# Attention-probability transposes by key block, and a new place for the text branch's small steps

## The chip, the cores and the metric

The kernel runs on one core of a Trainium2 chip. The metric is the device time of one execution in microseconds, the median over runs.

## What is computed

Two batches of 256 image tokens and 32 text tokens, width D = 1152, all in bf16. Each stream is normalised, scaled and shifted by rows that come from a condition vector, projected to Q, K and V with weights of its own, attended jointly over 288 keys with one head, projected out, gated and added to its input. Cut to what matters:

```
mod_i = (silu(c) @ wmod_img)   # six parts; the first three are used: shift, scale, gate
mod_t = (silu(c) @ wmod_txt)
hi = layernorm(x_img) * (1 + sci) + shi
ht = layernorm(x_txt) * (1 + sct) + sht
qkvi, qkvt = hi @ wqkv_img, ht @ wqkv_txt
q, k, v = [concatenate(text part, image part) for each]
p = softmax(q @ k.T * D**-0.5)
a = p @ v
out_i = x_img + gai * (a[image rows] @ wo_img)
out_t = x_txt + gat * (a[text rows] @ wo_txt)
```

## The kernel before

**Weights.** The fourteen weight blocks of 1152 x 1152 (2.65 MB each) pass through five slots of on-chip memory, `w0` to `w4`. A block that takes over a slot is loaded once all readers of the block before it are through, in the order of SyncE's queue (line 110 on). From the image scale on the order is: image scale (slot 0), image V (1), image shift (2), image Q (3), text shift (0), the text tokens, image K (4), text scale (1), text Q (2), four small `svb` loads, text K (3), image gate (0), text V (1), image O (4), text gate (3), text O (1). SyncE hands a DMA in only when its wait is over, and everything later in its queue stands behind it. `load_rows` hands in a block in pieces of rows, so that its first rows can be used before the last have landed.

**TensorE's order** is the order in which the program is written, since every matmul and transpose goes through `mm` or `tr`, which pin it. After the normalisation of the image tokens it is: image V, the image shift, the Shift-times-V rows (`shift_v_rows`: what the image shift contributes to V, as a row, added after attention as a bias), then image Q in nine column blocks and image K in nine (`qk_img`, 81 matmuls each). Text work hangs in hooks between those blocks: the text statistics and the text shift on VectorE, the transposes of the text tokens before K's second block, the text scale rows before K's fifth, text Q before K's ninth. Then come text K, the scores, the image gate row, text V, the transposes of P, attention, and the output.

**Shift-times-V rows.** `shift_v_rows` (line 403) makes 36 matmuls with image V's weights, ScalarE copies the rows to `svr` and stores them to a scratch in DRAM with two DMAs of its own; VectorE transposes them to columns (`svc`, the bias of the image part). Four DMAs of SyncE read the scratch back, broadcast over partitions, to `svb`, which text V's result subtracts.

**P and its transposes.** The softmax writes five tiles of 384 columns: two query tiles for each batch, and one for the text queries of both batches. VectorE writes the first 288 columns, GpSimd a second copy of the text keys further right, so that they come out on the partitions where text V's rows lie. `p_transposes` (line 628) is called for one batch and one or two key blocks at a time. It turns three tiles for each key block; for batch 1 the text tile is multiplied with `ident2`, an identity rotated by 32, since the text rows there stand first. ScalarE copies blocks 0 and 1, VectorE block 2, each into a tile of its own for each batch.

**Attention** (`attn_pair`, line 657) works on three column blocks of both batches at a time: the image keys of the first batch, the text keys of both, the image keys of the second.

**The output** has four image tiles of 128 tokens, three column chunks each (the last tile four), and one text tile. For each chunk VectorE multiplies by the gate from PSUM (`tmp`, two buffers) and adds the input. The text gate row (`txt_gate`) stands between the first and second chunk of image tile 1; it goes through ScalarE, a DRAM scratch and GpSimd's DMAs to `gbf`. The text tile (`out_txt`) stands before image tile 3.

Of the kernel before, what the change touches and what calls it, by code (L numbers as in the profile page):

```python
# [9 lines left out]
ALU = mybir.AluOpType  # L10
# [4 lines left out]
def kernel(  # L15
# [14 lines left out]
    nc = tc.nc  # L30
    bf = mybir.dt.bfloat16
    f32 = mybir.dt.float32
    PSUM = bass.MemoryType.PSUM

    B, NI, D = x_img.shape
    NT = x_txt.shape[1]
    P = 128
# [22 lines left out]
    def mm(*a, **k):  # L60
        return pin(nc.tensor.matmul(*a, **k))  # L61

    def tr(*a, **k):
        return pin(nc.tensor.transpose(*a, **k))  # L64
# [19 lines left out]
    def load_w(slot, src, c0, splits=(D,)):  # L84
        t = wtile(slot)
        sv = wview(src, c0)
        o = 0
        for n in splits:
            nc.sync.dma_start(t[:, :, o:o + n], sv[:, :, o:o + n])
            o += n  # L90
        return t

    def load_rows(slot, src, c0, cuts=(0, 3, 6)):
        t = wtile(slot)
        sv = wview(src, c0)
        for r0, r1 in zip(cuts, cuts[1:] + (KT,)):
            nc.sync.dma_start(t[:, r0:r1, :], sv[:, r0:r1, :])
        return t
# [14 lines left out]
    w_sh_t = load_rows(0, wmod_txt, 0, (0, 1, 3, 6))  # L113
    nc.sync.dma_start(x_t[:], xt_flat[:, :])
    w_k_i = load_w(4, wqkv_img, D)
    w_sc_t = load_w(1, wmod_txt, D)
    w_q_t = load_w(2, wqkv_txt, 0)

    nc.scalar.preload_act_table_set("natural_log_exp_and_others")
    eps_t = eps_row[:, 0:1]  # L120
# [27 lines left out]
    nc.gpsimd.memset(pb_txt, 0.0)  # L148
    nc.gpsimd.memset(xn_t[NTT:P, (KT - KH) * P:KH * P], 0.0)
    nc.gpsimd.memset(pb_all[:, 0:2 * B, NTOK:PBW], 0.0)  # L150
    ident2 = const.tile([P, P], bf)
    nc.gpsimd.tensor_copy(ident2[:, 0:P - NT], ident[:, NT:P])
    nc.gpsimd.tensor_copy(ident2[:, P - NT:P], ident[:, 0:NT])
    fold = const.tile([P, NGG, LW], bf)
    nc.vector.reduce_max(fold[:, 0, :], ident[:].rearrange("p (g l) -> p l g", g=NGG), axis=AX.X)
    nc.gpsimd.tensor_copy(fold[:, 1:NGG, :], fold[:, 0, :].unsqueeze(1).to_broadcast([P, NGG - 1, LW]))
# [228 lines left out]
    def qk_img(wq, blk, hooks):  # L385
        for j in range(KT):
            for hook in hooks.get(j, ()):
                hook()
            ps = ps_mm.tile([P, B * NI], f32, tag="mm")
            for kt in range(KT):  # L390
                mm(ps[:], lhsT=wq[:, kt, j * P:(j + 1) * P], rhs=hT_i[:, kt, :],
                   start=(kt == 0), stop=(kt == KT - 1))
            qk_evac(qkT[:, blk * KT + j, :, 0:NI], ps[:].rearrange("p (b n) -> p b n", b=B), blk)
# [9 lines left out]
    def shift_v_rows():  # L403
        p_sv = mod_rows_of(w_v_i, shT32)
        nc.scalar.copy(svr[:], p_sv[:])
        cols["v"] = mod_cols_of(p_sv, "svc")
        for b in range(B):
            nc.scalar.dma_start(svd[b].rearrange("(c g l) -> g c l", g=NGG, l=LW), svr[b:P:LW])
        for g in range(2):
            for b in range(B):  # L410
                r0 = 64 * g + NT * b
                nc.sync.dma_start(svb[r0:r0 + NT, :], svd[b, g * HD:(g + 1) * HD].partition_broadcast(NT))
# [84 lines left out]
    def qk_txt(blk, wq):  # L497
        for j0 in range(0, KT, FG):
            jn = min(FG, KT - j0)
            ps = ps_mm.tile([P, FG, NTT], f32, tag="mm")  # L500
            for j in range(j0, j0 + jn):
                for kt in range(KT):
                    mm(ps[:, j - j0, :], lhsT=wq[:, kt, j * P:(j + 1) * P], rhs=hT_t[:, kt, :],
                       start=(kt == 0), stop=(kt == KT - 1))
            qk_evac(qkT[:, blk * KT + j0:blk * KT + j0 + jn, :, NI:NTOK],
                    ps[:, 0:jn, :].rearrange("p j (b n) -> p j b n", b=B), blk)
# [52 lines left out]
    def txt_gate():  # L559
        mod_row_out(mod_rows(w_ga_t), 1)  # L560
        for g in range(2):
            for b in range(B):
# [2 lines left out]
                                    gsc[1, b, :].rearrange("(r g j) -> g r j", r=2, g=2)[g].partition_broadcast(NT))  # L565

    v_last()
    shift_v_rows()
    w_k_t = load_w(3, wqkv_txt, D)
    w_ga_i = load_w(0, wmod_img, 2 * D)  # L570
    w_v_t = load_w(1, wqkv_txt, 2 * D)
    w_o_i = load_rows(4, wo_img, 0)
    w_ga_t = load_w(3, wmod_txt, 2 * D)
    w_o_t = load_rows(1, wo_txt, 0, (0, 5))
    qk_img(w_q_i, 0, {0: (shift_part(0, 2),), 3: (txt_stats, shift_part(2, 4), txt_var, txt_norm),
                      5: (shift_part(4, 7),), 8: (shift_part(7, KT),)})
    qk_img(w_k_i, 1, {1: (txt_transposes,), 4: (txt_rows_scale, shift_blocks, txt_scale),
                      7: (shift_fold, txt_shift), 8: (lambda: qk_txt(0, w_q_t),)})
    qk_txt(1, w_k_t)

    aT = act.tile([P, KT, B * NTOK], bf, tag="Q")
    qpos = [[0, P, 2 * P], [NT, NT + P, 0]]
# [17 lines left out]
    def soft_div(key):  # L600
        sps, qn, nmx, e, rs = soft[key]
        pin(nc.vector.reciprocal(rs[0:qn, :], rs[0:qn, :]))  # L602
        pb = pb_txt if key == "t" else pb_tiles[key[0] * TPB + key[1]]
        pin(nc.vector.tensor_scalar_mul(pb[0:qn, 0:NTOK], e[0:qn, :], rs[0:qn, :]))
        pin(nc.gpsimd.tensor_scalar(pb[0:qn, NI + 2 * NT:NI + 3 * NT], e[0:qn, NI:NTOK], rs[0:qn, :], 0.0,  # L605
                                     op0=ALU.mult, op1=ALU.add))
        pbs[key] = pb

    def scores_img(b, qi):
# [13 lines left out]
                   start=(ft < 2), stop=(ft >= KT - 2), tile_position=(0, r0))  # L623
        return sps

    pTs = {}

    def p_transposes(b, kjs, pool, copy):
        pT_ps = pool.tile([P, 8 * P], bf, tag="tr" if pool is ps_tr else "mm", name="pT_ps")
        txt = [(2, pbs["t"], ident2 if b else ident)]  # L630
        img = [(qi, pbs[(b, qi)], ident) for qi in range(TPB)]
        for n, kj in enumerate(kjs):
            for qi, pb, perm in (txt + img if b else img + txt):
                o = n * NTOK + qpos[b][qi]
                k0 = kj * P - (NT * b if kj == 2 else 0)
                tr(pT_ps[:, o:o + P], pb[:, k0:k0 + P], perm[:])
        if b not in pTs:
            pTs[b] = work.tile([P, 3, NTOK], bf, tag="pT", name="pT")
        pin(copy(pTs[b][:, kjs[0]:kjs[-1] + 1, :],  # L639
                 pT_ps[:, 0:len(kjs) * NTOK].rearrange("p (k n) -> p k n", n=NTOK)))  # L640

    def attn_keys(tiles, first):
        for b, dt in tiles:
            for kj in range(2):
                mm(tiles[(b, dt)][:], lhsT=v_i[:, b * TPB + kj, dt * P:(dt + 1) * P], rhs=pTs[b][:, kj, :],
                   start=(first and kj == 0), stop=(not first and kj == 1))

    def attn_evac(tiles):
        for b, dt in tiles:
# [44 lines left out]
    gate_row()  # L694
    v_txt_out(0, vt[0])
    vt.append(v_txt(1))
    p_transposes(0, (0, 1), ps_tr, nc.scalar.copy)
    v_txt_out(1, vt[1])
    p_transposes(0, (2,), ps_mm, nc.vector.tensor_copy)
    p_transposes(1, (2,), ps_mm, nc.vector.tensor_copy)  # L700
    p_transposes(1, (0, 1), ps_tr, nc.scalar.copy)
    img_gate_spread()
    for dts in ((0, 5, 1), (6, 2, 7), (3, 8, 4)):
        attn_pair(*[[(b, dt) for dt in dts] for b in range(B)])

    def out_img(i, chunks, parts=None, between=None):
        b = i // TPB
        t0 = b * NTOK + qpos[b][i % TPB]
        o = work.tile([P, D], bf, tag="o")
        c0 = s0 = 0  # L710
        for n in chunks:
            if c0 and between:
                between = between()
            ps = ps_mm.tile([P, CH], f32, tag="mm")
            for dt in range(KT):
                mm(ps[:, 0:n], lhsT=aT[:, dt, t0:t0 + P], rhs=w_o_i[:, dt, c0:c0 + n],
                   start=(dt == 0), stop=(dt == KT - 1))
            tmp = work.tile([P, CH], bf, tag="tmp")
            nc.vector.tensor_mul(tmp[:, 0:n], ps[:, 0:n], gb[:, b, c0:c0 + n])  # L719
            nc.vector.tensor_add(o[:, c0:c0 + n], tmp[:, 0:n], x_i[:, i, c0:c0 + n])  # L720
            c0 += n
            if parts is None and c0 == D or parts and c0 in parts:
                (nc.scalar if parts and c0 == D else nc.sync).dma_start(oi_v[b, i % TPB, :, s0:c0], o[:, s0:c0])
                s0 = c0

    def out_txt():
        of = work.tile([P, 2, VC], bf, tag="of", bufs=1)
        for r in range(2):
            ps = ps_mm.tile([P, VC], f32, tag="mm")
            for dt in range(KT):  # L730
                for g in range(2):
                    c0 = (2 * r + g) * VC
                    mm(ps[64 * g:64 * g + NTT, :], lhsT=aT[:, dt, NI:NI + NTT], rhs=w_o_t[:, dt, c0:c0 + VC],
                       start=(dt == 0), stop=(dt == KT - 1), tile_position=(0, 64 * g))
            tmp = work.tile([P, CH], bf, tag="tmp")
            nc.vector.tensor_mul(tmp[:, 0:VC], ps[:], gbf[:, r, :])
            nc.vector.tensor_add(of[:, r, :], tmp[:, 0:VC], xf[:, r, :])
        for g in range(2):
            eng = nc.sync if g == 0 else nc.scalar
            eng.dma_start(ot_flat.rearrange("t (r g j) -> g t r j", r=2, g=2)[g], of[64 * g:64 * g + NTT, :, :])  # L740

    C3 = (CH, CH, CH)
    out_img(0, C3)
    out_img(1, C3, between=txt_gate)
    out_img(2, C3)
    out_txt()
    out_img(3, (CH, CH, 224, 160), parts=(2 * CH, D - 160, D))


# [28 lines left out]
```

## Time and profile before

| What | Value |
|---|---|
| median of 15 runs | 117.96 us (117.7 to 118.53) |
| profiled execution, its own time | 118.04 us |
| its span | 115.84 us |
| TensorE busy | 110.3 us (95% of the span) |
| VectorE busy | 72.1 us (62%) |
| ScalarE busy | 44.2 us (38%) |
| GpSimd busy | 12.4 us (11%) |
| moved by DMA | 41.02 MB, 354 GB/s over the span |

The span runs from the first to the last instruction of the profiled execution; its own time is 2.2 us longer, for what lies around it. Idle time of an engine costs nothing unless the last instruction waits for it in the end. Where one says that a transfer lands, it is the time at which the last of its DMA engines reports.

### The profile page before, as it was taken

To read this page: it belongs to the slowest core of one execution; us is meant where nothing else is said; L and a number is where in the kernel's file an instruction comes from. 1 tells how busy PE (TensorE), PEld (TensorE's weight loads), DVE (VectorE), ACT (ScalarE), POOL (GpSimd) and SP (SyncE) were. 2 spreads that over 40 slices of the span, in tenths; PEclk is the share of its full clock that TensorE was granted. 3 is DMA by queue.
4 is the path that set the end of the run, shared out by engine and by line. 5 is a ranking of instruction groups with operands and counts; after the bars stand their busy time and mean duration, and the time that the engine had idled before them with its cause. 6 is when DMAs were issued, how large, how long until landed. Compare 5 with 4: busy or idle time off the path is not lost.

```text
span 115.8 us, 2586 instructions
## 1 busy us (share of the span) xinstructions
PE 110.3 (95%) x1081; PEld 63.5 (55%) x1081; DVE 72.1 (62%) x152; ACT 44.2 (38%) x92; POOL 12.4 (11%) x34
## 2 busy tenths in 40 slices
PE   4998899999999999999999999999999999999990
PEld 2245544445674444445454458887866565557670
DVE  3489691063869999999996040018758509566671
ACT  5799800041752289825241233244657400100000
POOL 7300000000000000000000000003431600424000
PEclk9999999999999999999999999999999999999998
DMA  3999999999999999999999999999999999953223
GB/s 108 372 383 385 396 404 409 415 412 408 413 400 411 309 383 403 411 412 409 414 350 388 410 407 411 410 410 408 410 407 409 403 426 366 393 192 51 102 51 102
DMA packets 18917, 41.02 MB, mean 354 GB/s; under 512 B 1323, under 2 KB 1851, under 8 KB 18907
## 3 DMA queue, kind: packets, MB, share of 16 engines
q1 hardware_dynamic: 18032, 39.85, 89.9%
q0 software_dynamic: 480, 0.89, 2.5%
q10 hardware_dynamic: 395, 0.12, 0.4%
q8 instruction: 8, 0.13, 0.4%
q14 instruction: 2, 0.02, 0.0%
HBM read 39.52 MB, written 1.34 MB: 353 GB/s over the span
## 4 chain that ended last, share of the span: by engine, by line
PE 84%; ACT 5%; DVE 4%; DMA 3%; issue 1%; DVEq 0%
PE ps L61 52%; PE vps L61 15%; PE gps L61 5%; PE aps L61 5%; PE sps L61 4%; DMA x_i<-in_x_img_dram 3%; ACT xn_i L198 2%; ACT xn_i L197 2%; DVE tmp L719 1%; DVE xT_i L260 1%; DVE o L720 1%; PE tp L64 1%; ACT pT L639 1%; PE sc_ps L61 1%; DVE xn_i L212 0%
## 5 line engine op out<-in xcount | busy, mean ns | idle before, releaser
L61 PE MATMUL ps<-xT_i,t 128*128 128x512 bf16 x162 | 35.7, 379 | 0.0
L61 PEld LDWEIGHTS <-t 128*128 128x128 bf16 x333 | 20.9, 98 | 19.1 <-issue 0.7
L453 DVE SCALAR_TENSOR_TENSOR acc_sh<-t,sTf,acc_sh 128x1152 f32<-128x1152 bf16 x16 | 21.4, 1405 | 0.0
L61 PE MATMUL ps<-t,aT 128*128 128x384 bf16 (+3 forms) x153 | 20.3, 308 | 0.0
L61 PE MATMUL vps<-t,hS_i 128*128 128x512 bf16 (+1 forms) x108 | 17.9, 326 | 0.5 <-DVE scc L265 0.5
L61 PEld LDWEIGHTS <-aT 128*128 128x128 bf16 (+1 forms) x153 | 13.0, 101 | 7.1 <-issue 0.8
L61 PEld LDWEIGHTS <-hS_i 128*128 128x128 bf16 x108 | 9.1, 98 | 9.2 <-issue 0.5
L719 DVE TENSOR_TENSOR tmp<-ps,gb 128x384 bf16<-128x384 f32 (+2 forms) x13 | 6.8, 525 | 7.9 <-PE ps L61 4.3
L383 ACT CAST qkT<-ps 128x512 bf16<-128x512 f32 (+2 forms) x11 | 6.1, 552 | 14.8 <-PE ps L61 13.5
L605 POOL TENSOR_SCALAR pb<-e,rs 128x32 bf16<-128x32 f32 (+1 forms) x5 | 2.2, 445 | 75.8 <-DVE rs L602 75.8
L381 ACT ACTIVATE qkT<-ps 128x512 bf16<-128x512 f32 (+2 forms) x11 | 6.1, 561 | 8.3 <-PE ps L61 6.7
L61 PE MATMUL wps<-warm 128*128 128x512 bf16 x24 | 7.7, 479 | 1.5 <-DVE unit L127 1.5
L180 DVE CAST v_i<-vps 128x512 bf16<-128x512 f32 x5 | 3.5, 692 | 8.3 <-PE vps L61 8.3
L590 DVE TENSOR_REDUCE nmx<-sps 128x1 f32<-128x288 f32 x4 | 1.8, 457 | 9.4 <-PE sps L61 9.4
L182 ACT CAST v_i<-vps 128x512 bf16<-128x512 f32 x4 | 2.3, 580 | 10.3 <-PE vps L61 10.3
L652 DVE TENSOR_SCALAR aT<-aps,svc 128x288 bf16<-128x288 f32 x9 | 4.3, 517 | 2.2 <-PE aps L61 2.2
L61 PEld LDWEIGHTS <-sT 128*32 128x32 bf16 x180 | 4.5, 96 | 1.8 <-issue 1.2
L61 PEld LDWEIGHTS <-warm 128*128 128x128 bf16 x25 | 2.6, 114 | 5.0 <-issue 2.4
L61 PE MATMUL sps<-qkT 128*128 128x288 bf16 (+1 forms) x54 | 5.3, 287 | 0.0
L61 PE MATMUL gps<-t,sT 128*32 128x288 bf16 x144 | 5.2, 287 | 0.0
L61 PE MATMUL aps<-pT,v_i 128*128 128x288 bf16 x36 | 5.1, 287 | 0.1
L61 PE MATMUL ps<-hT_t,t 128*128 128x64 bf16 x162 | 5.0, 193 | 0.0
(114 smaller groups left out, 105.6 us busy)
## 6 DMA issues: line engine op xcount, KB each, us to landing
t<-in_wqkv_txt_dram SPq DMA_DIRECT2D x3, 2592.0 KB, 19.7
t<-in_wmod_img_dram SPq DMA_DIRECT2D x2, 2592.0 KB, 14.5
t<-in_wmod_txt_dram SPq DMA_DIRECT2D x2, 2592.0 KB, 18.8
t<-in_wqkv_img_dram SPq DMA_DIRECT2D x3, 864.0 KB, 13.5
t<-in_wqkv_img_dram SPq DMA_DIRECT2D x1, 2592.0 KB
t<-in_wo_img_dram SPq DMA_DIRECT2D x3, 864.0 KB, 10.4
t<-in_wqkv_img_dram SPq DMA_DIRECT2D x3, 576.0 KB, 10.6
t<-in_wmod_txt_dram SPq DMA_DIRECT2D x2, 864.0 KB, 13.0
```

The source lines that it names most:

```text
L61: return pin(nc.tensor.matmul(*a, **k))
L180: nc.vector.tensor_copy(out_ap, in_ap)
L182: nc.scalar.copy(out_ap, in_ap)
L197: pin(nc.scalar.activation(junk, x_ap, ACT.Copy, scale=1.0 / D, accum_out=sm[:, 0:1]))
L198: pin(nc.scalar.activation(junk, x_ap, ACT.Square, scale=float(D) ** -0.5, accum_out=sm[:, 1:2]))
L381: nc.scalar.mul(out_ap, in_ap, SCALE)
L383: nc.scalar.copy(out_ap, in_ap)
L453: pin(nc.vector.scalar_tensor_tensor(acc, w_sh_t[:, kt, :], col, acc, op0=ALU.mult, op1=ALU.add))
L590: pin(nc.vector.reduce_max(nmx[0:qn, :], sps[0:qn, :], axis=AX.X, negate=True))
L605: pin(nc.gpsimd.tensor_scalar(pb[0:qn, NI + 2 * NT:NI + 3 * NT], e[0:qn, NI:NTOK], rs[0:qn, :], 0.0, op0=ALU.mult, op1=ALU.add))
L652: nc.vector.tensor_scalar(dst, tiles[(b, dt)][:], bias, None, op0=ALU.add)
L719: nc.vector.tensor_mul(tmp[:, 0:n], ps[:, 0:n], gb[:, b, c0:c0 + n])
```

## The change

- **P's transposes** are made for one key block and both batches at a time, in one tile of 576 columns; the text tile is turned once for both batches, so that there are 15 and no `ident2`. Batch 1's first image tile overwrites the spare columns beside the text rows. For this the text tile holds its text keys three more times.
- **Copies** of the turned P go by batch halves: key block 0 of batch 0 by VectorE, block 1 of batch 0, then blocks 0 and 1 of batch 1 by ScalarE, block 2 as a whole by VectorE after the second text V result. In the first attention step the matmuls go over the key blocks first.
- **Shift-times-V rows** move from before image Q to before image K's fourth block, with the text scale rows, which come one block earlier. The slots change: text scale 2, text Q 3, text K 1, text V 2. Text K stands before the four `svb` loads in SyncE's queue; the image gate and what follows stand behind them. Text O comes in pieces of seven and two row blocks.
- **Text gate and text output** come after image tile 1: gate row, then the text matmuls in four column groups of 32 instead of two of 64, over the first seven row blocks of both halves and then the last two, into two PSUM tiles of the other pool. Their multiplications follow image tile 2, and GpSimd makes the two additions. VectorE's operations of the output are pinned in program order.

```diff
-    w_sc_t = load_w(1, wmod_txt, D)
-    w_q_t = load_w(2, wqkv_txt, 0)
+    w_sc_t = load_w(2, wmod_txt, D)
+    w_q_t = load_w(3, wqkv_txt, 0)
+    w_k_t = load_w(1, wqkv_txt, D)
...
-    shift_v_rows()
-    w_k_t = load_w(3, wqkv_txt, D)
-    w_ga_i = load_w(0, wmod_img, 2 * D)
-    w_v_t = load_w(1, wqkv_txt, 2 * D)
-    w_o_i = load_rows(4, wo_img, 0)
-    w_ga_t = load_w(3, wmod_txt, 2 * D)
-    w_o_t = load_rows(1, wo_txt, 0, (0, 5))
+    def late_loads():
+        late["ga_i"] = load_w(0, wmod_img, 2 * D)
+        late["v_t"] = load_w(2, wqkv_txt, 2 * D)
+        late["o_i"] = load_rows(4, wo_img, 0)
+        late["ga_t"] = load_w(3, wmod_txt, 2 * D)
+        late["o_t"] = load_rows(1, wo_txt, 0, (0, 7))
...
-    qk_img(w_k_i, 1, {1: (txt_transposes,), 4: (txt_rows_scale, shift_blocks, txt_scale),
+    qk_img(w_k_i, 1, {1: (txt_transposes,), 3: (shift_v_rows, txt_rows_scale, late_loads, shift_blocks, txt_scale),
...
-        pin(nc.gpsimd.tensor_scalar(pb[0:qn, NI + 2 * NT:NI + 3 * NT], e[0:qn, NI:NTOK], rs[0:qn, :], 0.0,
-                                     op0=ALU.mult, op1=ALU.add))
+        if key == "t":
+            dst, src = pb[0:qn, NTOK:PBW].rearrange("p (r k) -> p r k", k=NT), \
+                e[0:qn, NI:NTOK].unsqueeze(1).to_broadcast([qn, PBW // NT - NTOK // NT, NT])
+        else:
+            dst, src = pb[0:qn, NI + 2 * NT:NI + 3 * NT], e[0:qn, NI:NTOK]
+        pin(nc.gpsimd.tensor_scalar(dst, src, rs[0:qn, :], 0.0, op0=ALU.mult, op1=ALU.add))
...
+    def p_transposes(kj, pool):
+        ps = pool.tile([P, B * NTOK], bf, tag="tr" if pool is ps_tr else "mm", name="pT_ps")
+        k0 = kj * P
+        for pb, c0, o in [(pbs[(0, qi)], k0, qpos[0][qi]) for qi in range(TPB)] + [(pbs["t"], k0, NI)] + \
+                [(pbs[(1, qi)], k0 - (NT if kj == 2 else 0), NTOK + qpos[1][qi]) for qi in range(TPB)]:
+            tr(ps[:, o:o + P], pb[:, c0:c0 + P], ident[:])
+        return ps
+
+    def p_out(kj, ps, copy, b0=0, b1=B):
+        pin(copy(pT[:, kj, b0 * NTOK:b1 * NTOK], ps[:, b0 * NTOK:b1 * NTOK]))
...
-    p_transposes(0, (0, 1), ps_tr, nc.scalar.copy)
+    pt0, pt1, pt2 = p_transposes(0, ps_tr), p_transposes(1, ps_tr), p_transposes(2, ps_mm)
+    p_out(0, pt0, nc.vector.tensor_copy, 0, 1)
     v_txt_out(1, vt[1])
-    p_transposes(0, (2,), ps_mm, nc.vector.tensor_copy)
-    p_transposes(1, (2,), ps_mm, nc.vector.tensor_copy)
-    p_transposes(1, (0, 1), ps_tr, nc.scalar.copy)
+    p_out(1, pt1, nc.scalar.copy, 0, 1)
+    p_out(0, pt0, nc.scalar.copy, 1, B)
+    p_out(2, pt2, nc.vector.tensor_copy)
+    p_out(1, pt1, nc.scalar.copy, 1, B)
...
     def out_txt():
+        tiles = [ps_tr.tile([P, VC], f32, tag="tr", name="txo") for r in range(2)]
+        for d0, d1 in ((0, 7), (7, KT)):
+            for r, ps in enumerate(tiles):
+                for dt in range(d0, d1):
+                    for g in range(2):
+                        for b in range(B):
+                            c0, r0, t0 = (2 * r + g) * VC, 64 * g + NT * b, NI + NT * b
+                            mm(ps[r0:r0 + NT, :], lhsT=aT[:, dt, t0:t0 + NT], rhs=w_o_t[:, dt, c0:c0 + VC],
+                               start=(dt == 0), stop=(dt == KT - 1), tile_position=(0, r0))
+        return tiles
+
+    def out_txt_store(tiles):
...
+            pin(nc.vector.tensor_mul(tmp[:, 0:VC], ps[:], gbf[:, r, :]))
+            pin(nc.gpsimd.tensor_add(of[:, r, :], tmp[:, 0:VC], xf[:, r, :]))
...
     out_img(0, C3)
-    out_img(1, C3, between=txt_gate)
+    out_img(1, C3)
+    txt_gate()
+    txt = out_txt()
     out_img(2, C3)
-    out_txt()
+    out_txt_store(txt)
     out_img(3, (CH, CH, 224, 160), parts=(2 * CH, D - 160, D))
```

More of the change, by code (lines that the diff above doesn't have):

```diff
@@ L150 @@
     nc.gpsimd.memset(pb_all[:, 0:2 * B, NTOK:PBW], 0.0)
-    ident2 = const.tile([P, P], bf)
-    nc.gpsimd.tensor_copy(ident2[:, 0:P - NT], ident[:, NT:P])
-    nc.gpsimd.tensor_copy(ident2[:, P - NT:P], ident[:, 0:NT])
     fold = const.tile([P, NGG, LW], bf)
@@ L567 @@
     v_last()
-    shift_v_rows()
-    w_k_t = load_w(3, wqkv_txt, D)
-    w_ga_i = load_w(0, wmod_img, 2 * D)
-    w_v_t = load_w(1, wqkv_txt, 2 * D)
-    w_o_i = load_rows(4, wo_img, 0)
-    w_ga_t = load_w(3, wmod_txt, 2 * D)
-    w_o_t = load_rows(1, wo_txt, 0, (0, 5))
+    late = {}
+    def late_loads():
[4 more added lines that the diff above has]
+        late["o_t"] = load_rows(1, wo_txt, 0, (0, 7))
     qk_img(w_q_i, 0, {0: (shift_part(0, 2),), 3: (txt_stats, shift_part(2, 4), txt_var, txt_norm),
                       5: (shift_part(4, 7),), 8: (shift_part(7, KT),)})
-    qk_img(w_k_i, 1, {1: (txt_transposes,), 4: (txt_rows_scale, shift_blocks, txt_scale),
+    qk_img(w_k_i, 1, {1: (txt_transposes,), 3: (shift_v_rows, txt_rows_scale, late_loads, shift_blocks, txt_scale),
                       7: (shift_fold, txt_shift), 8: (lambda: qk_txt(0, w_q_t),)})
     qk_txt(1, w_k_t)
+    w_ga_i, w_v_t, w_o_i, w_ga_t, w_o_t = [late[k] for k in ("ga_i", "v_t", "o_i", "ga_t", "o_t")]
     aT = act.tile([P, KT, B * NTOK], bf, tag="Q")
@@ L624, in scores_txt @@
         return sps
[L626 to L640, printed above, removed]
-    def attn_keys(tiles, first):
[L643 to L646, printed above, removed]
+    pT = work.tile([P, 3, B * NTOK], bf, tag="pT", bufs=1, name="pT")
+    pTs = [pT[:, :, b * NTOK:(b + 1) * NTOK] for b in range(B)]
+    def p_transposes(kj, pool):
[7 more added lines that the diff above has]
+        pin(copy(pT[:, kj, b0 * NTOK:b1 * NTOK], ps[:, b0 * NTOK:b1 * NTOK]))
+    def attn_keys(tiles, first):
+        loop = [(kj, key) for kj in range(2) for key in tiles] if first else \
+            [(kj, key) for key in tiles for kj in range(2)]
+        for kj, (b, dt) in loop:
+            mm(tiles[(b, dt)][:], lhsT=v_i[:, b * TPB + kj, dt * P:(dt + 1) * P], rhs=pTs[b][:, kj, :],
+               start=(first and kj == 0), stop=(not first and kj == 1))
     def attn_evac(tiles):
@@ L704, with out_img @@
         attn_pair(*[[(b, dt) for dt in dts] for b in range(B)])
-    def out_img(i, chunks, parts=None, between=None):
+    def out_img(i, chunks, parts=None):
         b = i // TPB
@@ L711, in out_img @@
         for n in chunks:
-            if c0 and between:
-                between = between()
             ps = ps_mm.tile([P, CH], f32, tag="mm")
@@ L718, in out_img @@
             tmp = work.tile([P, CH], bf, tag="tmp")
-            nc.vector.tensor_mul(tmp[:, 0:n], ps[:, 0:n], gb[:, b, c0:c0 + n])
-            nc.vector.tensor_add(o[:, c0:c0 + n], tmp[:, 0:n], x_i[:, i, c0:c0 + n])
+            pin(nc.vector.tensor_mul(tmp[:, 0:n], ps[:, 0:n], gb[:, b, c0:c0 + n]))
+            pin(nc.vector.tensor_add(o[:, c0:c0 + n], tmp[:, 0:n], x_i[:, i, c0:c0 + n]))
             c0 += n
@@ L726, in out_txt @@
     def out_txt():
-        of = work.tile([P, 2, VC], bf, tag="of", bufs=1)
[L728 to L734, printed above, removed]
+        tiles = [ps_tr.tile([P, VC], f32, tag="tr", name="txo") for r in range(2)]
[9 more added lines that the diff above has]
+    def out_txt_store(tiles):
+        of = work.tile([P, 2, VC], bf, tag="of", bufs=1)
+        for r, ps in enumerate(tiles):
             tmp = work.tile([P, CH], bf, tag="tmp")
-            nc.vector.tensor_mul(tmp[:, 0:VC], ps[:], gbf[:, r, :])
-            nc.vector.tensor_add(of[:, r, :], tmp[:, 0:VC], xf[:, r, :])
+            pin(nc.vector.tensor_mul(tmp[:, 0:VC], ps[:], gbf[:, r, :]))
+            pin(nc.gpsimd.tensor_add(of[:, r, :], tmp[:, 0:VC], xf[:, r, :]))
         for g in range(2):
```

## The prediction

> **What bounds the kernel now.** I read the page first, for the share of each engine and the rate of the transfers.
>
> ```profile
> span 115.8 us, 2586 instructions
> PE 110.3 (95%) x1081; PEld 63.5 (55%) x1081; DVE 72.1 (62%) x152; ACT 44.2 (38%) x92; POOL 12.4 (11%) x34
> GB/s 108 372 383 385 396 404 409 415 412 408 413 400 411 309 383 403 411 412 409 414 350 388 410 407 411 410 410 408 410 407 409 403 426 366 393 192 51 102 51 102
> PE 84%; ACT 5%; DVE 4%; DMA 3%; issue 1%; DVEq 0%
> ```
>
> Two resources are full. TensorE works without a break from 14 to 112.7 us, so work moved inside its order is worth nothing by itself. The transfers run at 400 to 415 GB/s until about 102 us, so a hole in that stream delays everything behind it. The landing times of the trace show how little room there is: Text V's weights land at 80.95, and TensorE wants them at about 81.8. The first five row blocks of Text O's weights land at 99.57, all nine at 102.35.
>
> Next, the chain of waits where the change cuts: P's copies.
>
> ```profile
> 84.28 0.46 PE pT_ps L64 x6
> 84.74 0.02 issue
> 84.76 0.65 ACT pT L639
> 85.41 0.04 issue
> 85.45 5.94 PE aps L61 x54
> ```
>
> TensorE starts attention at 85.45, when ScalarE has copied batch 0 and when its own 18 transposes are over (84.22 plus 1.18 in the timeline). Both end together, so only shortening both helps.
>
> Then SyncE's queue in the timeline (start, duration, DMA):
>
> ```profile
> 34.43 3.14 SPq L89 DMA_DIRECT2D t<-in_wmod_txt_dram  x1
> 37.61 7.18 SPq L89 DMA_DIRECT2D t<-in_wqkv_txt_dram  x1
> 44.90 7.88 SPq L412 DMA_DIRECT2D svb<-sv_scratch  x4
> 52.88 0.39 SPq L89 DMA_DIRECT2D t<-in_wqkv_txt_dram  x1
> 58.20 0.39 SPq L89 DMA_DIRECT2D t<-in_wmod_img_dram  x1
> ```
>
> SyncE is far ahead: it hands in each load 8 us or more before the stream reaches it. Last, the timeline of the end on VectorE:
>
> ```profile
> 106.50 0.36 DVE L720 TENSOR_TENSOR o<-tmp,x_i 128x384 bf16<-128x384 bf16 x1
> 107.42 0.46 DVE L736 TENSOR_TENSOR tmp<-ps,gbf 128x288 bf16<-128x288 f32 x1 [0.55 <-DMA gbf<-mod_scratch]
> 107.91 0.31 DVE L737 TENSOR_TENSOR of<-tmp,xf 128x288 bf16<-128x288 bf16 x1
> 108.24 0.46 DVE L736 TENSOR_TENSOR tmp<-ps,gbf 128x288 bf16<-128x288 f32 x1
> 108.73 0.31 DVE L737 TENSOR_TENSOR of<-tmp,xf 128x288 bf16<-128x288 bf16 x1
> 109.81 0.56 DVE L719 TENSOR_TENSOR tmp<-ps,gb 128x384 bf16<-128x384 f32 x1 [0.76 <-PE ps L61]
> ```
>
> The text output's four operations sit under TensorE's text matmuls (105.80 to 108.13), and VectorE is idle again before the last image tile. TensorE ends at about 112.7, VectorE's last addition at 113.35.
>
> **What the Trainium skill says.** GPSIMD Engine Reference, Elementwise — side-by-side cycle accounting: a two-input operation costs about 2.6 cycles an element at 1.2 GHz. The trace of before has none on GpSimd. SBUF — State Buffer, Who interferes with whom: a VectorE instruction with two SBUF inputs and a GpSimd one that reads SBUF block each other; no run shows it yet. DMA: Bandwidth & Descriptors, Two DMAs through the same engine are not ordered: a DMA that reads what another wrote must wait for the completion semaphore. Here svb (L412) reads sv_scratch, and SyncE stands in that wait.
>
> **The change part by part.**
>
> 1. *Transposes and copies.* 18 transposes take 1.18 us, 0.066 each; 15 take 0.98 and end at 85.20. Batch 0's first half needs three of them and a VectorE copy of 0.30, ready by 84.9; the second half needs eight and a ScalarE copy of about 0.4 (640 ns for twice the columns), ready by 85.3. Three matmuls of 0.125 us lie between. The text block is copied whole by VectorE after all 15: 85.3 plus 0.6 gives 85.9 to 86.0, just when the first six matmuls end. Gain 0.20; bounds 0 (the text copy is late by 0.2) to 0.28. GpSimd's 96-column pad instead of 32 adds about 0.1 (its copies cost 200 ns for 32 columns, 257 for 96) and delays gb, for which VectorE waits until 95.5; TensorE has six PSUM tiles and first needs one back at 99.9, so this is nothing.
>
> 2. *Shift-times-V rows later, slots exchanged.* TensorE's 36 matmuls (1.22 us) move from 33.1 to behind three blocks of the K projection; TensorE's sum to 84.2 us is unchanged. The K projection's first matmul and the rest have their data (image Q's weights land at 33.25, needed at 34.4). The queue is what changes. Text Q's load now waits for slot 3, until the image Q projection ends at 50.7; the stream works on the text scale until 54.08, so nothing. Text K's load waits for slot 1, that is for the moved rows: 59.95 - 1.22 - 1.95 = 56.8 start, 58.0 end; the stream is at Text Q until about 60.5 (54.08 plus 6.4 for a load), so nothing. But behind it in SyncE's queue stand the four svb, which wait for the two sv_scratch stores. ScalarE copies svr at 58.1 to 58.5 and issues at 58.5 and 59.2. In the trace of before these stores landed 6.5 and 6.7 us after their issue (34.86 to 41.39, 35.52 to 42.25), with the stream full, as here. So they land at 65.1 and 65.9; four issues of 0.42 us end at 67.4, and the image gate's load (L570) is handed in at 67.4, its first packets 0.9 us later (102.50 to 103.35 for an output store): 68.3. Text K's packets end at about 66.4. Before, the slowest DMA engine began the gate's load at about 67.4 (67.88 less half a microsecond from last packet to landing). So all later loads come **0.7 us later**; bounds 0 (the stores take 5.5 us, with less ahead of them) and 1.2. VectorE's svc transpose now stands before the shift blocks at 58.5, and these end near 63.4 where shift_fold is at 67.0: nothing.
>
> 3. *What the late stream hits.* Text V at 80.95 + 0.7 = 81.65 against 81.8: nothing, up to 0.4 at the upper bound. Image O and the gates have 3 us and more. Text O: TensorE starts the output at 91.03, 54 matmuls of 0.165 us end at 99.94, the text gate's 36 at 101.16. Then seven row blocks are wanted. They land at 99.57 plus two blocks of 0.70 = 100.97, plus 0.7 = 101.67: a **stall of 0.5**; bounds 0 and 1.0. The last two blocks land at 103.05, needed at 103.4. The text matmuls themselves: 72 of 32 columns against 36 of 64; v_txt's 72 take 2.21 to 2.5 us, the 36 of before 2.33; I take equal, plus or minus 0.15.
>
> 4. *The end.* Text output's VectorE work moves from under TensorE's text matmuls to between image tiles 2 and 3. Image tile 2's last addition ends about 1.0 us after its matmuls: 101.16 + 0.4 + 2.33 + 4.45 + 1.0 = 109.35, taking the stall a little below its centre. Gate rows: from the end of the gate's matmuls to the last gbf landing it was 98.39 to 107.29 = 8.9; with the stream over the two round trips shorten, and I take 7.9: 109.05; bounds 108.4 and 110.0. So the two multiplications start at about T = 109.35. They take 0.46 each. The additions go to GpSimd. Price: 288 x 2.6 / 1.2 = 0.62 us, plus 0.17 of fixed cost (its 32-column copy at 200 ns, less 32 x 0.9): **0.8 us each**, an estimate from the GPSIMD page. Lower bound 0.43, at the rate of its one-input copies (0.9 ns a column); upper 1.2, if a VectorE addition of 0.36 holds it. There are two tmp buffers, and VectorE's next two multiplications wait for Pool. The first starts at T + 0.5 + 0.8 + 0.05; behind it stand 2 x 0.95 + 0.70 + 0.60 = 3.2 us of VectorE; and its addition waits about 0.2 for the second GpSimd addition at the shared port. End: T + 4.75 = 114.1. Without Pool it would be T + 0.98 + 3.2, which is about TensorE's end plus 0.65, as now. Cost of the hold 0.55; bounds 0 and 1.0.
>
> Sum against the profiled execution (span 115.84, its own time 118.04): -0.20 + 0.4 + 0.55, less 0.15 because the hold and the stall partly share the slack at the gate rows = **+0.6**, so 118.6. The profiled execution lies 0.08 above the median of the runs shown (117.96), so I predict **118.5**.
>
> **The rivals.**
>
> *B, faster: the queue keeps pace.* The sv_scratch stores land by 64.5 us, so the gate's load is handed in before Text K drains; Text O's seven blocks are there at 101.16, and GpSimd adds in 0.45 us or less. Then the transposes' 0.2 and up to 0.15 of the text matmuls remain: 117.7. For it: VectorE still has 1.4 us idle in the last 5.3, and the store's 6.5 us of before were issued while SyncE's own load was stuck (34.43 to 37.57). Against it: GpSimd's DMAs at 83.8 and 89.4 also took 4 us to their first packet under the full stream. It decides if T is at most 108.9 and the GpSimd addition at most 0.5. Chance 0.17.
>
> *C, they cancel:* stall 0.1, hold 0.2, gain 0.2: 118.0. Chance 0.18.
>
> *D, a larger hole:* stores of 7.5 us or an emptied queue that restarts slowly; gate, Text V and Text O are each 1.5 us late: 0.7 at Text V, 0.6 more at Text O, and the hold: 119.4. For it: nothing else feeds the stream meanwhile. Chance 0.15.
>
> The forecast has 0.50. A difference under 0.2% (0.24 us) is about what a measurement of this kernel can't tell from none. The forecast's own range is 118.2 to 118.9. Leaving out a tenth on each side of all cases gives 117.7 to 119.3. Faster 0.17, same 0.18, slower 0.65.
>
> **What would show it.** Right: DMA rate dipping at 66 to 68.5 us; TensorE idle before txo at 101 us, released by the Text O load; the L719 operations of the last tile released by POOL of; the last addition about 1.2 us after TensorE's end. Attention starting at 85.2. Wrong: a full stream at 67 us, txo without a wait, POOL additions below 0.5 us, or a wait before the text-key matmuls at 86 us, which I put at nothing.

## The result, and the profile after

| | before | changed |
|---|---|---|
| median | 117.90 us (117.61 to 118.53, 47 runs) | 121.00 us (120.07 to 123.19, 9 runs) |
| ratio of the times | | 1.026, 95% interval 1.024 to 1.028 |
| profiled execution, own time and span | 118.04, 115.84 us | 121.00, 118.9 us |

The change costs 3.1 us. The direction was forecast; the size was not: the forecast was 118.5 us, and its range ended at 119.3. Medians here and below are over all executions, while ratios leave out those that took over 1.5% longer than the fastest of the same kernel.

The page of the changed kernel, the lines that answer to those of before:

```profile
span 118.9 us, 2651 instructions
PE 111.7 (94%) x1114; PEld 64.3 (54%) x1114; DVE 71.9 (60%) x150; ACT 43.6 (37%) x93; POOL 13.5 (11%) x34
PEclk9999999999999999999999999999769999999999
GB/s 115 383 388 391 399 403 412 412 411 412 407 403 392 316 414 410 412 367 412 357 356 411 184 298 408 409 401 413 406 406 414 421 367 415 409 158 16 37 130 118
PE 63%; DMA 21%; ACT 5%; DVE 5%; POOL 2%; issue 2%; SPq 0%; DVEq 0%
```

Busy times hardly differ. The chain tells more: DMA has 21% of it instead of 3%, TensorE 63% instead of 84%. The rate falls to 184 and 298 GB/s in slices 23 and 24 (65.4 to 71.3 us). The chain of waits names the load, in its piece from that place to attention's end:

```profile
67.28 0.34 SPq L89
67.62 0.04 issue
67.67 16.17 DMA t<-in_wqkv_txt_dram
83.84 0.04 issue
83.88 3.55 PE ps L61 x72
87.43 1.40 PE pT_ps L64 x15
88.83 5.78 PE aps L61 x54
```

Text V's weights land at 83.84, 2.9 us later than before, and TensorE starts its 72 text-value matmuls only then. This is the wait that the prediction put at nothing. It stands in the view of waits (in all, times, longest):

```profile
PE ps L61 <- DMA t<-in_wqkv_txt_dram: 2.3, 1, 2.3
```

The same windows of both kernels show where the stream lost its time (columns: window, its length, then busy time and instructions of each engine, TensorE's clock, DMA share, GB/s). Before:

```profile
51.50:53.50 2.00, 2.00 (x11) 0.88 (x9) 2.00 (x3) 0.60 (x1) 0.00 (x0) 1.00 1.03 407
58.50:60.50 2.00, 2.00 (x28) 0.98 (x29) 2.00 (x2) 0.64 (x2) 0.00 (x0) 1.00 1.08 339
66.00:69.50 3.50, 3.50 (x34) 1.85 (x33) 1.22 (x3) 0.87 (x2) 0.00 (x0) 1.00 1.05 408
```

After:

```profile
51.50:53.50 2.00, 2.00 (x14) 1.06 (x13) 2.00 (x2) 1.15 (x3) 0.00 (x0) 1.00 0.98 341
58.50:60.50 2.00, 2.00 (x21) 0.83 (x10) 2.00 (x3) 0.00 (x0) 0.00 (x0) 1.00 0.88 264
66.00:69.50 3.50, 3.50 (x49) 2.13 (x47) 1.22 (x3) 1.17 (x2) 0.00 (x0) 1.00 0.58 130
```

Against 410 GB/s, a window loses its length times (1 - GB/s / 410). Before that is 0.01 + 0.35 + 0.02 = 0.38 us; after, 0.34 + 0.71 + 2.39 = 3.44. The difference of 3.06 us accounts for Text V's 2.9. The 0.35 us that the second window loses before is no late load, since Text K had been handed in at 52.88: the four svb reads run there, and the weight packets beside them take up to 136 ns instead of 93. In the changed kernel these reads run in the third window. Without what goes with them, the late loads themselves cost about 0.3, 0.7 and 1.9 us. The timeline of SyncE's queue shows what stood ahead of each hole:

```profile
50.40 7.71 SPq L89 DMA_DIRECT2D t<-in_wqkv_txt_dram  x2
64.00 3.13 SPq L410 DMA_DIRECT2D svb<-sv_scratch  x4
67.23 0.39 SPq L89 DMA_DIRECT2D t<-in_wmod_img_dram  x1
67.67 0.66 SPq L89 DMA_DIRECT2D t<-in_wqkv_txt_dram  x1
```

Before, SyncE handed in each load 8 us or more ahead. Here text Q is handed in at 50.40, when image Q is through with slot 3; text K at 57.74 (the second of the first row), when the moved rows are through with slot 1; the image gate at 67.23, after the svb loads. Each hole is one of these waits.

The end on VectorE, which answers to the last timeline of before (idle time and its releaser in brackets):

```profile
112.20 0.81 DVE L746 TENSOR_TENSOR tmp<-txo,gbf 128x288 bf16<-128x288 f32 x2
113.50 0.56 DVE L723 TENSOR_TENSOR tmp<-ps,gb 128x384 bf16<-128x384 f32 x1 [0.48 <-POOL of L747]
...
114.36 0.55 DVE L723 TENSOR_TENSOR tmp<-ps,gb 128x384 bf16<-128x384 f32 x1
...
116.19 0.24 DVE L724 TENSOR_TENSOR o<-tmp,x_i 128x160 bf16<-128x160 bf16 x1
```

VectorE does wait for GpSimd's addition, as foretold, for 0.48 us, but the whole stretch from the first multiplication to the last addition's end takes 116.43 - 112.20 = 4.23 us instead of 4.75.

### The profile page after: what moved, and what is told of

It reads as the page before. It is cut to its first block, busy times and chain, and to the rows that moved or that the text cites. A ratio compares the mean times of both kernels' runs of the same rounds, so it can differ in the third digit from the quotient of the medians.

```text
span 118.9 us, 2651 instructions
## 1 busy us (share of the span) xinstructions
PE 111.7 (94%) x1114; PEld 64.3 (54%) x1114; DVE 71.9 (60%) x150; ACT 43.6 (37%) x93; POOL 13.5 (11%) x34
## 4 chain that ended last, share of the span: by engine, by line
PE 63%; DMA 21%; ACT 5%; DVE 5%; POOL 2%; issue 2%; SPq 0%; DVEq 0%
PE ps L61 37%; PE vps L61 15%; DMA t<-in_wqkv_txt_dram 14%; PE aps L61 5%; PE gps L61 4%; DMA x_i<-in_x_img_dram 3%; DMA mod_scratch<-g_sb 2%; ACT xn_i L195 2%; ACT xn_i L196 2%; DMA gbf<-mod_scratch 2%; DVE tmp L723 1%; PE pT_ps L64 1%; POOL gbf L562 1%; DVE xT_i L258 1%; DVE o L724 1%
## 5 line engine op out<-in xcount | busy, mean ns | idle before, releaser
L61 PE MATMUL ps<-t,aT 128*128 128x384 bf16 (+2 forms) x117 | 17.9, 314 | 0.0
L61 PE MATMUL ps<-t,hT_t 128*32 128x288 bf16 x72 | 3.5, 373 | 2.3 <-DMA t<-in_wqkv_txt_dram 2.3
```

## The experiments

My theory after the result: the rows part starves the stream. It makes SyncE hand in three loads too late, these holes delay Text V and Text O, and the other two parts of the change matter little. The rivals: the text gate and output part costs most of it (a late Text O, GpSimd's hold, narrow matmuls); or the transposes and copies do; or the low TensorE clock that the profiled execution shows. "Lost" below is the stream's loss between 49 and 84 us, worked out from the packets of the trace as bytes missing against 412 GB/s; it was 0.72 us before and 3.73 after. Each ratio is taken against executions of the kernel before that were made alongside.

### The rows and the queue alone

Edit on the kernel before: this part of the change only, Text O in seven and two row blocks included.

```diff
-    w_sc_t = load_w(1, wmod_txt, D)
-    w_q_t = load_w(2, wqkv_txt, 0)
+    w_sc_t = load_w(2, wmod_txt, D)
+    w_q_t = load_w(3, wqkv_txt, 0)
+    w_k_t = load_w(1, wqkv_txt, D)
...
-    shift_v_rows()
...
+    qk_img(w_k_i, 1, {1: (txt_transposes,), 3: (shift_v_rows, txt_rows_scale, late_loads, shift_blocks, txt_scale),
```

> The kernel before with the Shift-times-V rows moved and the slots exchanged, and nothing else. Theory S (holes in the stream of loads): the image gate's load is handed in at about 67.2 us behind the four svb loads, Text V lands near 83.8 instead of 80.95, TensorE waits over 2 us for it; 120.7 to 121.2. Rival T (the text output's late steps cost the time): 117.8 to 118.3, since they are as before here.

Measured: median 120.73 us, ratio 1.0171 (1.0138 to 1.0204). The four executions took 119.65, 120.00, 121.47 and 121.66 us. The ratio rests on the two shorter; the trace is of the 121.47 one and is read for its waits only. It lost 4.54 us of the stream in the same three places, Text V landed at 85.4, and the view of waits has it:

```profile
PE ps L61 <- DMA t<-in_wqkv_txt_dram: 3.2, 1, 3.2
```

This part alone costs 2.0 us by the ratio, less than the 2.8 to 3.3 that I expected, and 2.9 by the medians. Four executions don't decide between the two.

### The svb loads behind the weights

Edit on the changed kernel: the four svb loads follow the image gate and Text V in SyncE's queue.

```diff
+    def svb_loads():
...
         late["v_t"] = load_w(2, wqkv_txt, 2 * D)
+        svb_loads()
```

> The changed kernel with the four svb loads behind the image gate's and Text V's in SyncE's queue. Theory S: the hole at 66 to 69.5 us closes, Text V lands near 81.4, TensorE's wait for it falls under 0.3 us and the granted clock stays full; 118.0 to 118.7. Rival T: still 120.5 or more.

Measured: 120.03 us, ratio 1.0206 (1.0159 to 1.0253): only 1.0 us better than the changed kernel by the medians and 0.6 by the ratios, whose intervals overlap, where I expected 2.3 or more. The last hole did close (390 GB/s from 66 to 69.5 instead of 130), and the wait for Text V fell to 0.7 us. But the other two holes stayed, and a new one came at 79.5 to 83 us (336 GB/s), where the svb packets now ran and where SyncE handed in the text gate only at 82.53. The time came back at Text O:

```profile
PE txo L61 <- DMA t<-in_wo_txt_dram: 1.8, 1, 1.8
PE ps L61 <- DMA t<-in_wqkv_txt_dram: 0.7, 1, 0.7
```

So SyncE's stand at svb is one part of the cost, and a loss that is moved behind Text V is paid at Text O.

### The rows at their old place, slots as changed

Edit on the changed kernel:

```diff
+    shift_v_rows()
...
-    qk_img(w_k_i, 1, {1: (txt_transposes,), 3: (shift_v_rows, txt_rows_scale, late_loads, shift_blocks, txt_scale),
+    qk_img(w_k_i, 1, {1: (txt_transposes,), 3: (txt_rows_scale, late_loads, shift_blocks, txt_scale),
```

> The changed kernel with the Shift-times-V rows back ahead of image Q, slots and queue as changed. Slot 1 is then free early and the sv_scratch stores land long before SyncE comes to the svb loads, so two of the three places where the stream ran short (58.5 to 60.5, worth 0.75 us, and 66 to 69.5, worth 2.45 us) should be full; text Q's wait for slot 3 at 51.5 (0.37 us) stays. If these holes are the cause: Text V's weights land at 83.84 - 3.2 = 80.6 (81.4 with the svb reads' own time), TensorE waits for them at most 0.2 us, 118.0 to 118.6. If TensorE's order or the clock is the cause instead: a wait or a low clock stays, over 120.

Measured: 119.15 us, ratio 1.0100 (1.0079 to 1.0121), a miss above. As expected the second hole was gone (412 GB/s from 58.5 to 60.5) and the third nearly (353 GB/s; the 0.5 us that is still lost there goes with the svb reads, which run in it). But the first grew, which I had overlooked: with the rows ahead of it, image Q gives up slot 3 some 1.2 us later, text Q is handed in at 51.87 instead of 50.40, and the stream does this:

```profile
51.50:54.50 3.00, 3.00 (x19) 1.51 (x18) 3.00 (x3) 1.28 (x3) 0.00 (x0) 1.00 0.71 209
58.50:60.50 2.00, 2.00 (x31) 1.02 (x20) 2.00 (x2) 0.07 (x1) 0.00 (x0) 1.00 1.04 412
```

Lost: 2.23 us; Text V at 82.67 with a wait of 0.8, Text O 0.9. The slot exchange costs by itself: text Q's wait for slot 3, called nothing in the prediction, makes the first hole, which the kernels with the old slots below don't have (407 GB/s from 51.5 to 53.5 in the last of them).

### The svb loads on GpSimd's queue

Edit on the changed kernel:

```diff
-                nc.sync.dma_start(svb[r0:r0 + NT, :], svd[b, g * HD:(g + 1) * HD].partition_broadcast(NT))
+                nc.gpsimd.dma_start(svb[r0:r0 + NT, :], svd[b, g * HD:(g + 1) * HD].partition_broadcast(NT))
```

> The changed kernel with the four svb loads on GpSimd's queue, so that SyncE doesn't stand at them; the rows stay late. The hole at 66 to 69.5 should go, those at 51.5 and 58.5 (1.1 us together) stay. If the holes add up: Text V's weights land at about 82.0, TensorE waits up to 0.5 us there and up to 0.6 for Text O; 118.8 to 119.8, between the kernel with the rows early and the changed one. If SyncE's stand at svb is not what costs: 120.5 to 121.3.

Measured: 119.40 us, ratio 1.0104 (1.0025 to 1.0183); lost 2.44 us, 387 GB/s from 66 to 69.5. Waits: 0.8 us at Text V (it landed at 82.97, a microsecond later than expected; half of that is the rate, which stayed at 383 GB/s from 70 to 78), 1.1 at Text O. With the rows late and SyncE free, 1.6 us of the 3.1 are back by the medians and 1.8 by the ratios. That is the share of SyncE's stand at svb, as far as four executions tell; the interval is 0.9 us wide to either side.

### The text gate and output alone

Edit on the kernel before: this part of the change only (Text O still loaded in five and four row blocks).

```diff
     out_img(0, C3)
-    out_img(1, C3, between=txt_gate)
+    out_img(1, C3)
+    txt_gate()
+    txt = out_txt()
     out_img(2, C3)
-    out_txt()
+    out_txt_store(txt)
```

> The kernel before with the text gate and text output after image tile 1 and the additions on GpSimd, and nothing else. Theory S with the small tail that the prediction worked out: the last addition comes up to 0.6 us later behind TensorE; 118.0 to 118.6. Rival T: 120 or more. If the hold costs nothing: 117.7 to 118.0.

Measured: 118.52 us, ratio 1.0050 (1.0030 to 1.0069). TensorE waits 0.4 us for Text O, and the last addition ends 0.7 us after TensorE, as before. That wait is for all nine row blocks, since the matmuls ask for seven of a load that comes as five and four; the two runs on the pieces below separate that.

### The same with VectorE's additions

```diff
-            pin(nc.gpsimd.tensor_add(of[:, r, :], tmp[:, 0:VC], xf[:, r, :]))
+            pin(nc.vector.tensor_add(of[:, r, :], tmp[:, 0:VC], xf[:, r, :]))
```

> The kernel before with the text gate and output part alone, and its two additions on VectorE instead of GpSimd. If GpSimd's additions hold VectorE by 0.55 us as predicted: 0.5 us less than with GpSimd, about 118.0. If the hold is about 0.05, as the trace of the GpSimd version reads (the last addition 0.68 us after TensorE's end): within 0.3 of 118.5, and possibly more, since VectorE then has 0.6 us more to do in the tail.

Measured: 118.27 us, ratio 1.0015 (0.9995 to 1.0036). The intervals of this run and the last overlap, and the timelines differ by 0.1 us: from the first gated multiplication to the end 4.34 us on VectorE, 4.22 with GpSimd. GpSimd's hold is therefore no loss against the same additions on VectorE. Whether the 0.25 us between the medians is real stays open.

### The transposes and copies of P alone

Edit on the kernel before: `p_transposes`, `p_out`, the text tile's spare keys and the first attention step over the key blocks first, as in the change.

> The kernel before with the new transposes and copies of P, and nothing else. Theory: attention starts 0.2 us earlier; 117.6 to 117.8. Rival P (the copies by halves make attention wait for the text block): 118.0 to 118.4, with a wait before the text-key matmuls.

Measured: 117.43 us (117.01 to 118.04), ratio 0.9968 (0.9955 to 0.9982): a gain of 0.4 us, faster than both kernels. The chain from the transposes to attention's end:

```profile
84.36 0.94 PE pT_ps L64 x15
85.30 5.81 PE aps L61 x54
91.11 5.85 PE ps L61 x36
```

That is 6.75 us for 7.11 before (84.28 to 91.39). No copy stands between the transposes and attention any more, and within attention nothing is late either. TensorE's timeline shows where the gain lies, first before, then here:

```profile
84.22 1.18 PE L64 MATMUL pT_ps<-ident,pb 128*128 128x128 bf16 x18
85.45 0.90 PE L61 MATMUL aps<-pT,v_i 128*128 128x288 bf16 x6
```

```profile
84.29 1.01 PE L64 MATMUL pT_ps<-ident,pb 128*128 128x128 bf16 x15
85.15 0.91 PE L61 MATMUL aps<-pT,v_i 128*128 128x288 bf16 x6
```

From the first transpose to attention it is 0.86 us for 1.23. Attention itself, up to the first output matmul, is unchanged (5.80 us for 5.78).

### The change without the rows part

Edit on the changed kernel: rows, slots and queue as before, Text O in five and four row blocks.

> The changed kernel with the rows' place, the slots and SyncE's queue of the kernel before; the transposes and copies of P and the text gate and output as changed. If the parts add up: before - 0.4 + 0.6, that is 117.9 to 118.3, with a wait for Text O of about 0.8 us, since attention ends 0.4 earlier. If the parts interact (transposes hide the late Text O or the reverse): under 117.6 or over 118.8.

Measured: 118.34 us, ratio 1.0025 (1.0006 to 1.0045), lost 0.73 us as before. TensorE waits 0.8 us for Text O in the midst of its text matmuls, as expected. Two variants ask if that wait is the text part's cost. In the first the matmuls go over the blocks as loaded:

```diff
-        for d0, d1 in ((0, 7), (7, KT)):
+        for d0, d1 in ((0, 5), (5, KT)):
```

> The changed kernel without the rows part, as two runs earlier (118.34), but the text output's matmuls go over the first five row blocks of both halves and then the last four, as the two loads of Text O are cut there. There TensorE stood 0.8 us after 20 of the 72 matmuls, for the second load; now 40 stand before that point, 0.67 us more of cover. If the wait for Text O is what the text part costs: wait 0.1 to 0.2, 117.6 to 117.8. If the cost is elsewhere (32-column matmuls, the order of the tail): 118.2 or more.

Measured: 117.38 us (117.15 to 118.14), ratio 0.9957 (0.9935 to 0.9980), better than both kernels. Its wait is 0.5 us where I expected 0.1 to 0.2, because TensorE came earlier in this execution (to its text matmuls at 100.58 instead of 101.24):

```profile
100.58 1.40 PE L61 MATMUL txo<-t,aT 128*32 128x288 bf16 x40
102.50 1.16 PE L61 MATMUL txo<-t,aT 128*32 128x288 bf16 x32 [0.53 <-DMA t<-in_wo_txt_dram]
```

In the second, Text O is loaded as in the changed kernel:

```diff
-    w_o_t = load_rows(1, wo_txt, 0, (0, 5))
+    w_o_t = load_rows(1, wo_txt, 0, (0, 7))
```

> The changed kernel without the rows part, with Text O loaded in seven and two row blocks as in the changed kernel. Seven blocks land at about 101.4 where nine land at 102.8, and TensorE asks for them at 101.2 to 102. If the wait for Text O is what the text part costs: wait at most 0.3, 117.6 to 117.9. If not: 118.2 or more.

Measured: 118.02 us, ratio 1.0012 (0.9993 to 1.0031), between the two expectations. TensorE has no wait for Text O; instead the two multiplications wait 0.4 us for the gate rows:

```profile
109.15 0.82 DVE L742 TENSOR_TENSOR tmp<-txo,gbf 128x288 bf16<-128x288 f32 x2 [0.39 <-DMA gbf<-mod_scratch]
```

Both spans are alike (115.9 and 115.8 us), so why the medians are 0.6 us apart isn't settled by one trace of each. Nor is the wait for Text O the whole of what the first variant gains: it is shorter by 0.3 us, the median by 1.0. This last kernel differs from the changed one in the rows part alone (place, slots and queue). So that part costs 121.00 - 118.02 = 3.0 us of the 3.1, and the other two together cost next to nothing: 0.4 us gained by the transposes, about 0.5 lost by the text part. Why the rows part costs 3.0 us here and 2.0 by its ratio when it stands alone is not shown.

### The changed kernel once more

> The changed kernel unaltered, one more execution with a profile. In the profile at hand the TensorE clock fell to 0.50 for three microseconds after the wait for Text V, and Text O was no longer late. If that was a matter of one execution: full clock throughout, the 72 text-value matmuls in 2.3 to 2.4 us, Text V's weights landing 2.5 to 3.2 us later than before, and a wait of 1 us or more for Text O in place of the slow clock; 120 to 121. If the low clock belongs to the kernel: it comes back at 84 to 88 us.

Measured: 120.99 us in one execution, at full clock from 82 to 91 us and everywhere else. The waits:

```profile
PE ps L61 <- DMA t<-in_wqkv_txt_dram: 2.5, 1, 2.5
PE txo L61 <- DMA t<-in_wo_txt_dram: 0.9, 1, 0.9
```

In the first profiled execution TensorE ran its 72 text-value matmuls and the transposes at clock 0.50; that hid the wait for Text O, which landed at 103.89 while the text matmuls started at 104.42. Here the clock stayed up, TensorE arrived earlier and waited for Text O. Both executions took 121.0 us. Of the ten executions of the changed kernel whose clock was recorded before this one, eight have a mean clock of 1.00, and their median is 121.0 us as well. So the late stream sets the time either way, and the low clock is not its cause.

## Why the prediction was wrong

- **Step 2, text Q's slot: "so nothing".** It was wrong. The sum took the landing of the text scale as the moment at which the stream would run dry. But the 16 DMA engines finish a load far apart: in the changed kernel's trace the text scale's reports come between 52.10 and 53.73. Text Q, handed in at 50.40, came too late for the first of them, and the window lost 0.33 us more than before; with the rows early, 1.5 us. The six traces with the changed slots agree: between 51 and 55 us the stream loses 0.24, 0.34, 0.59, 0.40, 0.94 and 1.50 us where text Q is handed in 1.93, 1.70, 1.38, 1.33 and 0.79 us ahead of the text scale's first report and, in the last, 0.07 behind it.
- **Step 2, text K's slot: "so nothing".** The same mistake. Text K was handed in at 57.74 where the reports of text Q come from 59.03 to 60.17. The window lost 0.71 us, 0.36 more than before, when the svb reads ran in it.
- **Step 2, "all later loads 0.7 us later".** The mechanism was right, and the rate did dip from 66 us as foretold: SyncE stood at svb, and the gate's load was handed in at 67.23 (predicted 67.4), although sv_scratch's stores landed at 63.99 and 64.94 instead of 65.1 and 65.9; the svb issues took longer than the 0.42 us each that I took, up to 1.33. The first packets of the gate's load come at 68.29 (predicted 68.3). The size was not right, for two reasons. The sum measured the delay at the DMA engine that was through last, at 67.4, but the rate falls from 66.0 on as one engine after another runs out: by 68.25 the stream has lost 1.5 us, some of it with the svb reads. And the sum let the stream run at full rate from the first packet on, but from 68.25 to 69.5, while the first weight packets are slow, another 0.9 us is lost. Full rate is back about 69.5 to 70, over 2.3 us after the hand-in, and the window has lost 2.4 us. The excess of all three holes is 3.06 us where the step had 0.7. This is the term that carries the error. The step's upper bound of 1.2 left no room for it, so the range missed too.
- **Step 3, Text V: "nothing (up to 0.4)".** With the load 2.9 us late TensorE waited 2.3 us. The prediction's sign of being wrong, a wait before the text-key matmuls at 86 us, is another one, inside attention, and it did not come.
- **Step 3, Text O: "a stall of 0.5".** 0.9 in the second execution, 0 in the first, where the slow clock stood in its place. Most of the loss had already been paid at Text V.
- **Step 1, gain 0.20.** Direction right, 0.36 in the chain and 0.43 in the median. Three transposes less give 0.17 us (1.01 for 1.18). The other 0.2 us is ScalarE's copy: before, attention started at 85.45, 0.05 us after the last transpose's end in the timeline; without the copy in its way it starts 0.15 us ahead of that end. I had read copy and transposes as ending together, so that the copy alone cost nothing.
- **Step 4, additions of 0.8 us.** 0.73 for one alone (1.42 for both in the timeline). The Trainium skill's price, GPSIMD Engine Reference, Elementwise — side-by-side cycle accounting, 0.62 us by that step's working, with 0.17 of fixed cost from the trace, was good to 0.06.
- **Step 4, hold 0.55.** VectorE is released 1.30 us after T, as worked out (1.35). But what stands behind takes 2.93 us, not 3.2 plus 0.2 for the port: the starts of successive multiplications are 0.87 apart, not 0.95, since the next multiplication starts before an addition has ended (114.36 and 114.45). The addition that was to wait 0.2 us at the shared port takes 0.36 us, as elsewhere. And the comparison was at fault: without GpSimd the additions fall on VectorE at the same place, which came to 4.34 us against 4.22. So of the forecast's +0.6, the 0.55 of this term did not come: the direction came out right through the rows part alone.
- **The rivals.** D named the right mechanism, "an emptied queue that restarts slowly", but gave it 1.5 us and a chance of 0.15. Its other ground, stores of 7.5 us, did not come: they took 5.8 and 6.1. C and B fall: no part gave time enough to cancel 3 us.

In sum, on the second execution: +2.5 at Text V, +0.9 at Text O, -0.5 between the text-value matmuls' start and attention's (3.18 us for 3.65) make +2.9, which is the whole of 116.28 - 113.35 = 2.9 us between the last additions.

## What to carry to other kernels

When loads run back to back, look at when the earliest DMA engine reports the load ahead, not the last; here a hand-in 1.3 us ahead of that first report still left a hole of 0.7 us, one 7.9 us ahead left none, and a queue that ran empty cost about 1.9 us. A small load that depends on fresh results doesn't belong ahead of the big ones in one in-order queue. And take a change apart: here 0.4 us of gain lay in it, under 3.0 us of loss from another of its parts and 0.5 from the third; the transposes alone (117.43 us) or with the text output cut as its weights are loaded (117.38 us) are both faster than the kernel before, and their intervals overlap.

## What was not expected of the hardware

- TensorE's clock fell to 0.50 in the profiled execution, 1.1 us after a wait of 2.3 us had ended. In the windows of one microsecond the clock is 0.50 from 85 to 88 us and lower in part from 84 to 85 and from 88 to 89 (0.97 and 0.82), some 3.4 us in all. One more execution of the changed kernel (123.19 us) has the same mean clock of 0.986, and so has one of the rows part alone:

```profile
84.00:85.00 1.00, 1.00 (x36) 0.85 (x33) 0.00 (x0) 0.00 (x0) 0.67 (x2) 0.97 1.03 392
85.00:86.00 1.00, 1.00 (x24) 0.68 (x16) 0.68 (x2) 0.00 (x0) 0.00 (x0) 0.50 1.04 410
...
88.00:89.00 1.00, 1.00 (x14) 0.95 (x13) 0.85 (x3) 0.41 (x2) 0.10 (x1) 0.82 1.05 408
```

  The Trainium skill (TensorE: Matmul & The Clock Gate, Part 1: The HAM clock gate) has a free-running window of about 3.4 us, after which an idle TensorE drops to half clock and a busy one comes back. The length agrees; but the gap was shorter than a window, while waits of 2.5 and 3.2 us in other executions left the clock at 1.00. What decides it stays open.
- After an empty stretch even the packets are slow: between 66.5 and 69.5 us the 91 weight packets of the changed kernel took 222 ns each on average, where 522 in the same stretch of the kernel before took 94. The svb reads beside them are not needed for it: in the kernel with the rows early and the slots as changed, the 61 weight packets from 52.75 to 53.75 us, with no svb read among them, took 215 ns. Why they are slow stays open.
